# A convolution and a gated two-layer product on one core: the joins of the first product over both PSUM banks of a pair at once

## The chip, the cores and the metric

The kernel runs on one core of a Trainium2 chip. Five engines work side by side, each in the order of its own instruction list, and wait for each other through counters (semaphores): TensorE (PE, matrix products; its weight loads are listed apart as PEld), VectorE (DVE), ScalarE (ACT), GpSimd (POOL) and SyncE (SP), which here only starts transfers. PE writes its results into PSUM, which has eight banks of 512 fp32 values in each of 128 partitions. DVE and ACT read and write PSUM, and everything else lies in SBUF.

The metric is the device time of one execution in microseconds: the median of several runs. Lower is better.

## The reference

```python
# lightweight convolution: batch 8, sequence 4096, width 192, 8 heads of 24 channels, 7 taps
w = softmax(weight, axis=-1)                       # [8, 7]
x_pad = concatenate([zeros(B, 6, D), x], axis=1)
out[b, s, h*24+g] = sum_k w[h, k] * x_pad[b, s+k, h*24+g]
# two-layer product with a quick GELU, over all 32768 tokens
h = out.reshape(32768, 192) @ w_in                 # w_in [192, 2048]
g = h * (1 / (1 + exp(-1.702 * h)))
result = g @ w_out                                 # w_out [2048, 192]
```

All of it is fp32, and a matrix product of fp32 operands runs as two passes on PE, so each product is two records in the profile.

## The kernel before

The tokens are worked in 32 big steps. Each holds two column blocks of 512 tokens (one from each half of the batch). A big step has a first product (tokens by `w_in`, then the GELU) and a second product (the result by `w_out`). Both use schemes of the Strassen kind, which need fewer block products and pay with sums of blocks. Big step 0 is done by functions of its own (`first_step`, with `plain` and `second_first`) while the weights are still being loaded and rounded; big steps 1 to 31 all run through the same two functions, `hidden` (called twice, for `v` = 0 and 1) and `second`. Nothing is scheduled by a planner of times: the order of each engine's list is the order in which the code issues it (`manual_schedule`). The waits between engines are put in by the framework, from the tiles that each instruction reads and writes.

**PSUM.** The eight banks are eight tiles of 128x512: `slots`, three pairs, and `sums`, one pair. In the code a pair is a list of two tiles, one for each `h`. The names `x`, `y`, `z` and `sums` move round among the four pairs from step to step.

**First product** (`hidden`). `terms` calls `product1` (L616) 21 times for each `v`. Each call issues two matmuls, one into each bank of a pair; they use different halves of PE's rows and run together. Between them `copy2` (L653) copies a pair from PSUM to one of five SBUF buffers `k15`, `k16`, `k18`, `k19`, `k20` (all in the tile `room`) as two ACT copies, one for each bank. `sum2` (L657) joins a pair with one of these buffers: a VectorE sum or difference of two operands, done bank by bank as two operations of 128x512. There are six calls of `sum2` in each `hidden`: `x = z - k15`, `k15 = y - k19`, `k19 = z - k19`, `k20 = k20 + sums`, `k16 = y - k16`, `k18 = k18 + sums`. `gelu` writes the activation into the tile `g`: from a pair in PSUM as two operations (L638), from a buffer as one of 128x1024 (L642). Where `hidden` calls `work`, DVE does steps of the next token block's convolution (L502, L504); `sum_g` puts sums of blocks of `g` (L391, L393) on DVE.

**Second product** (`second`). `PLAN` lists it step by step. Here the two banks of a pair have different duties:

```python
mains, sides = (bs[0], bx[0], by[0]), (bx[1], bs[1], by[1])
```

A main product fills partitions 0 to 95 of a bank `mains[i]`, in three matmuls of 32 columns for every step of the sum; these are the values `p0` to `p5`, two to a bank. With every three of them goes one matmul of a side product, on PE's last 32 columns: it fills partitions 96 to 127 of a bank `sides[i]`. All four run together (`one_matmul`, L991). Seven side products of three chunks each make 21 side results, and each is copied to `room` by ACT as soon as its last matmul is done (L1016, 32x256). `seed` copies a main value to or from PSUM on ACT (L1020, 96x256), `join` adds or subtracts such values on DVE (L391, L393, 96x256), and `turn` transposes results into the output buffer (L908). So in this stage the bank with `h` = 0 of each pair holds main values and the bank with `h` = 1 side values.

**Big step 0.** `first_conv` (L1078) makes two thirds of the first convolution on PE in the pairs `slots[1]` and `slots[2]`, bank 0 for the first 512 tokens and bank 1 for the second. `take_straight` (L1092) and `take_across` (L1096) copy them out, and `split_rest` (L356, L357) follows on ACT on the way to the first rounded weights (L376). `second_first` uses the banks one by one, mains in `slots[1][0]`, sides in `sums[0]`, `sums[1]` and `slots[0][0]` (L822, L827; side copies L829).

Of the kernel before, what the change touches and what calls it, by code (L numbers as in the profile page):

```python
# [8 lines left out]
F32 = mybir.dt.float32  # L9
# [6 lines left out]
def kernel(  # L16
# [35 lines left out]
    P = 128  # L52
# [6 lines left out]
    TOK = 2 * T  # L59
# [17 lines left out]
    psum = ctx.enter_context(tc.tile_pool(name="psum", bufs=1, space=bass.MemoryType.PSUM))  # L77
# [9 lines left out]
    def load_x(big, ns=range(2)):  # L87
# [16 lines left out]
                    )  # L104


    slots = [
        [psum.tile([P, TOK], F32, name=f"slot{i}{h}") for h in range(2)] for i in range(3)
    ]
    sums = [psum.tile([P, TOK], F32, name=f"sums{h}") for h in range(2)]  # L110

# [534 lines left out]
    def bank(t, h):  # L648
        return t[h] if isinstance(t, list) else t[:, h, :]
# [3 lines left out]
            act.copy(bank(dst, h), bank(src, h))  # L653

    def sum2(op, dst, a, b):
        for h in range(2):
            op(*(bank(t, h) for t in (dst, a, b)))  # L657

    def plain(u, m, n, v, slot, ks=range(NC), first=0):

# [3 lines left out]
    def hidden(big, v, x, z, y, sums, work, fetch, last=lambda: None):  # L664
# [45 lines left out]

        pe(y, 6, 14, first=True)
        sum2(vec.tensor_sub, x, z, k15)
        early(1)
        if not v or big == 1:
# [6 lines left out]
        pe(z, 11)  # L721
        pe(sums, 20, 10)
        sum2(vec.tensor_sub, k15, y, k19)
        gelu(B12, 0, v, sums)
        pe(x, 4)
        copy2(k20, x)
        sum2(vec.tensor_sub, k19, z, k19)
        early(2)
        if not v or big == 1:
# [523 lines left out]
    for big in range(1, N_BIG):  # L1253
        more = big + 1 < N_BIG
        last = hidden(big, 0, x, z, y, sums, work, lambda: fetch(big, 1, z))
        x, z, y, sums = z, x, sums, y
# [39 lines left out]
```

## Time and profile before

| what | value |
|---|---|
| median of 3 runs | 2274.22 us (2273.69 to 2274.6) |
| profiled execution: span from the first to the last instruction | 2272.6 us; no other time is listed for it, and the median run is 1.6 us above the span |
| PE busy | 2263.4 us (100% of the span), granted clock 1.000 |
| DVE busy | 1941.0 us (85%) |
| ACT busy | 1568.8 us (69%) |
| POOL busy | 847.0 us (37%) |
| DMA | mean 125 GB/s |

Engines overlap, so the busy times don't add up. A row of a group of instructions gives the line, the engine, the operation, `written<-read` by tile names, shapes, count, then busy time, the mean in ns, and the idle time of the engine just before. A row of the timeline gives the start, the duration, engine, line, operation and count, and in brackets the engine's idle time before it with what ended it. All eight PSUM banks are called `slot` or `sums` there, without their numbers.

### The profile page before, as it was taken

The numbers are of one execution on the slowest core, as the hardware profiler recorded it, in microseconds if no ns is written. First come the engines' busy times: TensorE is split into PE (matmuls) and PEld (weight loads), VectorE is DVE, ScalarE is ACT, GpSimd is POOL, SyncE is SP. The second block draws the span as 40 slices with busy tenths as digits, with TensorE's granted clock in tenths as the row PEclk, the third lists the DMA queues.
The fourth block names the chain that finished last, engine by engine and source line by source line (L and its number), as shares of the span: only waits on it lengthen the run. The fifth ranks groups of instructions, "written<-read, shape, count | busy, mean of one in ns | idle before, by whom it ended". The sixth has DMA issues, their size and how long they took to land.

```text
span 2272.6 us, 60950 instructions
## 1 busy us (share of the span) xinstructions
PE 2263.4 (100%) x25214; PEld 1214.9 (53%) x25214; DVE 1941.0 (85%) x2794; ACT 1568.8 (69%) x2972; POOL 847.0 (37%) x834
## 2 busy tenths in 40 slices
PE   9999999999999999999999999999999999999998
PEld 5475555555555555555555555555555555555556
DVE  8998888888888888888888888888888888888877
ACT  8866776667766667666677666776667766667754
POOL 1544443244442344433444324444244442344400
PEclk9999999999999999999999999999999999999999
DMA  9976656656566665666655675656666566664443
GB/s 205 155 146 127 127 111 126 137 122 131 116 126 129 123 139 114 116 126 134 134 120 109 126 144 121 131 112 127 132 126 136 112 124 126 129 139 86 88 99 71
DMA packets 269908, 284.20 MB, mean 125 GB/s; under 512 B 117952, under 2 KB 206016, under 8 KB 269632
## 3 DMA queue, kind: packets, MB, share of 16 engines
q0 software_dynamic: 57648, 150.69, 36.9%
q1 hardware_dynamic: 210336, 129.22, 25.2%
q8 instruction: 199, 3.26, 0.6%
q14 instruction: 77, 0.63, 0.1%
q10 hardware_dynamic: 1648, 0.39, 0.1%
HBM read 53.15 MB, written 25.17 MB: 34 GB/s over the span
## 4 chain that ended last, share of the span: by engine, by line
PE 99%; DVE 1%; ACT 0%; DMA 0%; issue 0%; SPq 0%; ACTq 0%; DVEq 0%
PE slot L616 35%; PE slot L991 33%; PE sums L616 16%; PE sums L991 13%; PE slot L822 2%; DMA xin<-in_x_dram 0%; DVE room L657 0%; DVE xt L473 0%; ACT conv_t L1096 0%; DVE conv_t L504 0%; SPq L99 0%; ACT conv_t L357 0%; DVE room L393 0%; ACT conv_t L356 0%; DVE g L391 0%
## 5 line engine op out<-in xcount | busy, mean ns | idle before, releaser
L616 PE MATMUL slot<-conv_t,w_in_s 64*128 64x512 f32 x3740 | 862.5, 591 | 0.3 <-DVE w_in_s L376 0.3
L991 PE MATMUL slot<-g,w_form 128*32 128x256 f32 x7024 | 710.8, 379 | 0.4 <-DVE room L657 0.4
L616 PEld LDWEIGHTS slot<-conv_t,w_in_s 64*128 64x128 f32 x3740 | 377.6, 187 | 423.9 <-issue 347.7
L393 DVE TENSOR_TENSOR g<-g 128x1024 f32<-128x1024 f32 x372 | 448.9, 1234 | 3.2
L991 PEld LDWEIGHTS slot<-g,w_form 128*32 128x32 f32 x7024 | 375.7, 110 | 118.1 <-DVE room L657 0.9
L616 PE MATMUL sums<-conv_t,w_in_s 64*128 64x512 f32 x1660 | 408.3, 589 | 0.3 <-DVE w_in_s L376 0.3
L1016 ACT COPY room<-slot 32x256 f32<-32x256 f32 x434 | 159.3, 367 | 310.3 <-PE slot L991 309.2
L642 ACT ACTIVATE g<-room 128x1024 f32<-128x1024 f32 x310 | 325.7, 1077 | 67.9 <-DVE room L657 67.9
L991 PE MATMUL sums<-g,w_form 128*32 128x256 f32 x2648 | 368.8, 379 | 0.0
L991 PE MATMUL slot<-g,w_out_s 128*32 128x256 f32 x4080 | 318.8, 380 | 0.0
L967 POOL DMA_DIRECT2D g<-g x124 | 106.2, 857 | 496.6 <-PE slot L991 156.8
L616 PEld LDWEIGHTS sums<-conv_t,w_in_s 64*128 64x128 f32 x1660 | 172.1, 187 | 184.9 <-issue 140.0
L518 POOL TENSOR_TENSOR conv_t<-conv_t,g 128x512 f32<-128x512 f32 x180 | 262.2, 1457 | 16.3 <-POOL conv_t L518 3.0
L530 POOL DMA_DIRECT2D g<-g x120 | 105.5, 879 | 422.5 <-PE sums L991 128.7
L653 ACT COPY room<-slot 128x512 f32<-128x512 f32 x434 | 231.4, 601 | 38.5 <-PE slot L616 38.4
L516 ACT ACTIVATE g<-xt,cw 128x512 f32<-128x512 f32 x360 | 248.5, 730 | 2.2
L991 PEld LDWEIGHTS slot<-g,w_out_s 128*32 128x32 f32 x4080 | 164.7, 110 | 128.5 <-ACT g L638 22.7
L638 ACT ACTIVATE g<-slot 128x512 f32<-128x512 f32 x334 | 180.8, 598 | 45.4 <-PE slot L616 24.8
L991 PEld LDWEIGHTS sums<-g,w_form 128*32 128x32 f32 x2648 | 177.9, 110 | 37.6
L504 DVE SCALAR_TENSOR_TENSOR conv_t<-xt,cw,conv_t 128x512 f32<-128x512 f32 (+1 forms) x198 | 192.0, 970 | 4.6
L393 POOL TENSOR_TENSOR conv_t<-conv_t 128x256 f32<-128x256 f32 x180 | 181.9, 1024 | 9.4
L1016 ACT COPY room<-sums 32x256 f32<-32x256 f32 x217 | 79.6, 367 | 145.0 <-PE sums L991 142.5
(205 smaller groups left out, 2909.5 us busy)
## 6 DMA issues: line engine op xcount, KB each, us to landing
g<-g POOLq DMA_DIRECT2D x124, 512.0 KB, 5.8
xin<-in_x_dram SPq DMA_DIRECT2D x240, 180.0 KB, 4.3
conv_t<-conv_t SPq DMA_DIRECT2D x180, 192.0 KB, 3.1
g<-g POOLq DMA_DIRECT2D x120, 256.0 KB, 3.8
out_dram<-osbs SPq DMA_DIRECT2D x186, 128.0 KB, 4.9
g<-room POOLq DMA_DIRECT2D x31, 512.0 KB, 5.3
conv_t<-g POOLq DMA_DIRECT2D x60, 256.0 KB, 4.8
g<-osbs POOLq DMA_DIRECT2D x30, 512.0 KB, 4.7
```

The source lines that it names most:

```text
L393: eng.tensor_sub(v(dst), v(a), v(b))
L504: vec.scalar_tensor_tensor(out=dst, in0=src, scalar=tap, in1=dst, op0=ALU.mult, op1=ALU.add)
L516: act.mul(home, conv_src(big, c, k), cw[:, c, k : k + 1])
L518: nc.gpsimd.tensor_add(dst, dst, home)
L530: nc.gpsimd.dma_start(out=out, in_=src, accum_op=ALU.add)
L616: nc.tensor.matmul(slot[h], w_in_s[halves[h], a, v * P : (v + 1) * P], src, start=first, stop=True, skip_group_check=True,)
L638: act.activation(dst[:, :, h, :], src[h].rearrange("p (o t) -> p o t", o=2), AF.Gelu_apprx_sigmoid)
L642: act.activation(dst.rearrange("p o h t -> p h o t"), src.rearrange("p h (o t) -> p h o t", o=2), AF.Gelu_apprx_sigmoid,)
L653: act.copy(bank(dst, h), bank(src, h))
L967: nc.gpsimd.dma_start(out=spot(dst), in_=spot(a), accum_op=ALU.add)
L991: nc.tensor.matmul(dst, w, t, start=first, stop=last, skip_group_check=True)
L1016: act.copy(to, d)
```

## The change

Each PSUM pair becomes one tile of 128x2x512 that holds both banks. It is still a list of the two banks for all code that takes them one at a time, and has a view of both. `sum2` uses that view, and so issues one VectorE operation of 128x1024 where it issued two of 128x512.

```diff
-    slots = [
-        [psum.tile([P, TOK], F32, name=f"slot{i}{h}") for h in range(2)] for i in range(3)
-    ]
-    sums = [psum.tile([P, TOK], F32, name=f"sums{h}") for h in range(2)]
+    class Banks(list):
+
+        def __init__(self, name):
+            tile = psum.tile([P, 2, TOK], F32, name=name)
+            super().__init__(tile[:, h, :] for h in range(2))
+            self.both = tile[:, :, :]
+
+    slots = [Banks(f"slot{i}") for i in range(3)]
+    sums = Banks("sums")
...
     def sum2(op, dst, a, b):
-        for h in range(2):
-            op(*(bank(t, h) for t in (dst, a, b)))
+        op(*(t.both if isinstance(t, Banks) else t for t in (dst, a, b)))
```

The instructions of PE, ACT, POOL and SP stay the same in number and order. DVE loses one instruction for each call of `sum2` (2 x 6 calls in each of 31 big steps, 372 in all). What else changes is the list of waits: the tiles are now four in place of eight. Lines below the change move by 4 or 5 (L616 becomes L621, L657 becomes L661, L991 becomes L995).

## The prediction

> **What bounds the kernel.** I read the page's busy times and its chain first, then the busy times by stage, then the timeline of one big step.
>
> ```profile
> span 2272.6 us, 60950 instructions
> PE 2263.4 (100%) x25214; PEld 1214.9 (53%) x25214; DVE 1941.0 (85%) x2794; ACT 1568.8 (69%) x2972; POOL 847.0 (37%) x834
> ...
> PE 99%; DVE 1%; ACT 0%; DMA 0%; issue 0%; SPq 0%; ACTq 0%; DVEq 0%
> ```
> ```profile
> core 0: us, PE busy (x) PEld busy (x) DVE busy (x) ACT busy (x) POOL busy (x), PEclk, DMA share, GB/s
> 0.00:18.00 18.00, 15.43 (x154) 11.76 (x154) 12.24 (x36) 13.70 (x36) 3.12 (x16) 1.00 0.99 211
> 1006.26:1042.51 36.25, 36.25 (x172) 16.70 (x169) 30.75 (x41) 30.39 (x51) 18.58 (x17) 1.00 0.59 114
> 1042.51:1076.32 33.81, 33.81 (x627) 20.18 (x625) 30.06 (x44) 18.18 (x42) 7.73 (x9) 1.00 0.68 138
> ```
>
> The chain is PE for 99%. The last two rows are the two stages of one big step (first product, second product): PE is busy for 36.25 of 36.25 and 33.81 of 33.81 us. So the other engines are paced by PE. Two things follow: work saved on DVE can't shorten a big step, and any time for which PE is made to wait lengthens the run by just that, 31 times.
>
> **The fused joins on DVE.**
>
> ```profile
> core 0: us, DVE busy (x), PEclk, DMA share, GB/s
> 0.00:2272.60 2272.60, 466.76 (x744) 1.00 0.63 125
> ```
> ```profile
> L393 DVE TENSOR_TENSOR g<-g 128x1024 f32<-128x1024 f32 x372 | 448.9, 1234 | 3.2
> ```
>
> The 744 joins of L657 overlap slightly: 466.76 / 744 = 0.627 us of busy time each, so a pair costs 1.255. There is no 128x1024 operation with a PSUM operand in the trace. The nearest row is the SBUF sum of 128x1024, 1.234 us, and I take it. The upper end is what a pair costs now, 1.255; as a lower end I take a fifth less than the row, 1.0, since no row of that size is near it. The saving is then 372 x 0.02 = 8 us of DVE time, at most 372 x 0.25 = 93, and I price it at nothing: PE's own work covers it. If PE were not busy all the time, it would be a gain of that size at most.
>
> The join as one also starts later. It needs both halves of what it waits for, and ACT delivers these one after the other.
>
> ```profile
> 1028.07 1.08 ACT L638 ACTIVATE g<-slot 128x512 f32<-128x512 f32 x2 [0.69 <-issue]
> ...
> 1028.70 1.30 DVE L657 TENSOR_TENSOR slot<-slot,room 128x512 f32<-128x512 f32 x2 [1.01 <-ACT g L638]
> ...
> 1031.26 1.88 PE L616 MATMUL slot<-conv_t,w_in_s 64*128 64x512 f32 x8
> ...
> 1033.24 2.47 DVE L657 TENSOR_TENSOR room<-slot,room 128x512 f32<-128x512 f32 x4
> ...
> 1034.69 1.88 PE L616 MATMUL slot<-conv_t,w_in_s 64*128 64x512 f32 x8
> ```
>
> Now the first half starts at 1028.70, as soon as the first activation is done, and the pair ends at 1030.00. In one piece it starts at 1028.07 + 1.08 = 1029.15 and ends at 1030.38, 0.4 later. PE needs that slot at 1031.26, so 0.9 is left of 1.3. Behind it on DVE are queued the sums of `g` and then the four joins from 1033.24; the first two end at 1034.5 and PE needs their slot in the second half of the row from 1034.69, at 1035.55. With 0.4 to 0.6 of delay 0.4 is still left, more than the 0.19 of a weight load. Where PE's result is what the join waits for, nothing is later at all. I price the joins' delay at 0 and keep 0.2 us a big step as its upper end.
>
> **The tiles.** The second part of the diff is the larger one. The built order of the changed kernel, with its waits, has the waits by tile: whoever writes one bank of a pair waits for whoever reads the other, and the reverse. In the first product that changes nothing, since both banks are used by the same two operations. In the second product the two banks of a pair hold different things, mains and sides. I took the waits of one second product as the changed kernel has them, and looked up in the timeline of before when each awaited instruction ends. Eleven matmuls of L991 start there before what they would have to wait for has ended. Each is a stop of PE. They are of four kinds.
>
> *Five times, mains behind a side copy of their own pair.* The first and the last:
>
> ```profile
> 1045.79 0.38 PE L991 MATMUL sums<-g,w_form 128*32 128x256 f32 x1
> 1045.99 0.39 PE L991 MATMUL sums<-g,w_out_s 128*32 128x256 f32 x3
> ...
> 1046.24 0.37 ACT L1016 COPY room<-sums 32x256 f32<-32x256 f32 x1 [0.86 <-PE sums L991]
> 1046.62 0.35 ACT L1020 COPY slot<-slot 96x256 f32<-96x256 f32 x1
> ...
> 1046.65 0.38 PE L991 MATMUL slot<-g,w_form 128*32 128x256 f32 x1
> ...
> 1046.87 0.38 PE L991 MATMUL slot<-g,w_form 128*32 128x256 f32 x1
> ```
> ```profile
> 1072.77 0.38 PE L991 MATMUL sums<-g,w_form 128*32 128x256 f32 x1
> ...
> 1073.00 0.37 ACT L1016 COPY room<-slot 32x256 f32<-32x256 f32 x1 [0.59 <-PE slot L991]
> ```
>
> A side ends with the matmul of 1045.79. PE goes on at 1045.99 with mains in the other bank of the same pair. As one tile they wait for the copy, 1046.24 + 0.37 = 1046.61: 0.62 late. The last: 1073.37 against the group of 1072.77, 0.6. To that comes PE's restart. Before has such a stop in its first second product:
>
> ```profile
> 135.87 0.37 ACT L1020 COPY room<-slot 96x256 f32<-96x256 f32 x1
> ...
> 136.29 0.42 PE L991 MATMUL slot<-osbs,w_form 128*32 128x256 f32 x3
> ...
> 136.53 0.82 PE L991 MATMUL slot<-osbs,w_form 128*32 128x256 f32 x11
> ```
>
> The copy ends at 136.24, PE starts at 136.29, and its next pass comes 0.24 after that in place of the 0.21 to 0.22 elsewhere: 0.05 + 0.03 = 0.08. So 0.70 each, 5 x 0.70 = 3.5 us.
>
> *Once, the same with a copy that is late already.*
>
> ```profile
> 1044.28 0.38 PE L991 MATMUL sums<-g,w_form 128*32 128x256 f32 x1
> ...
> 1045.01 0.37 ACT L1016 COPY room<-slot 32x256 f32<-32x256 f32 x1
> ```
>
> The copy ends at 1045.38, and the mains of the group of 1044.28 need its pair: 1.1 + 0.08 = 1.2.
>
> *Twice, a side behind a seed copy that itself has to wait.* The copy of 1046.62 (`seed`) reads one bank of a pair whose other bank a side is still filling. As one tile it waits for the matmul of 1046.65, which ends at 1047.03, and ends at 1047.4; the next matmul of a side in that pair is that of 1046.87: 0.55 + 0.08, with its twin 1.3 together.
>
> *Three times, a side behind a join on DVE.*
>
> ```profile
> 1060.09 0.87 DVE L393 TENSOR_TENSOR room<-room,slot 96x256 f32<-96x256 f32 x2
> ...
> 1060.91 0.37 ACT L1016 COPY room<-slot 32x256 f32<-32x256 f32 x1 [0.47 <-PE slot L991]
> ...
> 1061.12 0.38 PE L991 MATMUL slot<-g,w_form 128*32 128x256 f32 x1
> ...
> 1062.01 0.41 DVE L391 TENSOR_TENSOR room<-sums,room 96x256 f32<-96x256 f32 x1
> ...
> 1062.63 0.38 PE L991 MATMUL sums<-g,w_form 128*32 128x256 f32 x1
> ...
> 1062.84 0.38 PE L991 MATMUL sums<-g,w_form 128*32 128x256 f32 x1
> ```
>
> The two joins of 1060.09 can start only after the copy of 1060.91, at 1061.28, and end at 1062.15; the side of 1061.12 waits for them, 1.0 + 0.08. The join of 1062.01 waits for the matmul of 1062.63 (1063.01) and ends at 1063.42; the side of 1062.84 waits, 0.6 + 0.08. The third is like the second. Together 2.5.
>
> Sum: 3.5 + 1.2 + 1.3 + 2.5 = 8.5 us for each second product; 31 of them, 264 us. What else waits on ACT, DVE and POOL for these comes later by no more than PE itself.
>
> Bounds: if the restart cost nothing and the three joins were covered, 11 stops become 8 of 0.6 and one longer by 0.5, 5.3 us or 165 in all; if two more of the 21 side copies came to stop PE, 8.5 + 1.4 + the 0.2 of the joins, 10.1 us or 313.
>
> **Big step 0.**
>
> ```profile
> 9.87 0.37 ACT L1092 COPY conv_t<-slot 128x256 f32<-128x256 f32 x1 [0.63 <-PE slot L1078]
> ...
> 10.52 0.51 ACT L356 ACTIVATE conv_t<-conv_t,bias 128x256 f32<-128x256 uint32 x1 [0.28 <-DVE conv_t L345]
> ...
> 13.14 3.70 PE L616 MATMUL slot<-conv_t,w_in_s 64*128 64x512 f32 x16
> ```
> ```profile
> 83.52 0.57 ACT L829 COPY room<-sums 32x512 f32<-32x512 f32 x1
> ```
>
> The copy of 9.87 takes the first 512 tokens out of a pair while PE fills its other bank until about 13.1; as one tile it waits for that, and the weights of L616 wait behind it on ACT (L356): up to 3 us, less what was to spare, 2.5. In `second_first` four copies like that of 83.52 become stops of about 1 us each, 4. Together 6.5, between 0 and 10.
>
> **Sum.** 2272.6 + 264 + 6.5 = 2543 for the span, and the runs' median stands 1.6 above the span: 2545 us, 12% slower.
>
> **Rivals.** *PE's clock falls.* Eleven stops in 34 us could make the throttle grant less. If a quarter of each second product ran at half clock, that is 31 x 33.81 / 4 = 262 us more: 2807. Against it: the stretch from 0 to 18 us has PE busy for 15.43 of 18.00, and its granted clock is 1.00. [...] 3%.
>
> *All side copies stop PE.* There are 21 in each second product. If the delays shift them against each other so that the other ten count too, 31 x 10 x 0.70 = 217 more: 2762. Against it: the stops delay mains and sides alike. 5%.
>
> *The waits are met in time, and the kernel is not slower.* This is so if the copies end before PE gets to the matmuls behind them. Then the most to be had is a few us of PE's idle time, 2272.6 - 2263.4 = 9.2, nearly all of it in the start; I set it at 2272. It decides at one place: the copy of 1046.24 would have to end 0.62 us sooner, that is before it starts. That the framework tells the two banks of a tile apart, so that no wait is added, comes to the same time, and the built order speaks against it. 4% for both.
>
> **Numbers.** The forecast has 88%. 2545 is its sum. Its bounds are 2274 + 165 + 0 = 2439 and 2274 + 313 + 10 = 2597; the low end takes covers that the timeline does not show, so I put it at 2490, and the high end at 2600. That leaves out the three rivals and little else. A measurement of this kernel tells about 0.2% from no change. Slower by over 0.2%: 96%; within 0.2%: 2%; faster: 2%.
>
> **What would show it.** Each big step takes 78.6 in place of 70.06 us, all of it in the second product, which goes from 33.8 to about 42.3; the first stays at 36.25. L1016 ACT copies and L391/L393 joins of 96x256 appear as what ends the idle time of PE and PEld on L991, 31 times each. PE's busy share falls to about 90%, at a granted clock of 1.00. The joins (L661) are 372 of about 1.23 us. Wrong would be the forecast if second products stayed near 34 us, if the first product grew, or if the clock dropped.

## The result, and the profile after

The changed kernel takes 2548.36 us (median of its runs, 2547.64 to 2550.05) against 2274.22 before: a ratio of 1.1207, with a 95% interval of 1.1191 to 1.1223. It is 12% slower; the forecast was 2545. One execution of a kernel told of below, the convolution laid out by token halves, took 4241.75 us at a mean granted clock of 0.556; it is left out of that kernel's median (2547.94 with it) and of its ratio.

The page of the kernel after, the lines that answer to those shown of before (span, busy times, shares of the chain by engine):

```profile
span 2546.1 us, 60733 instructions
PE 2377.6 (93%) x25214; PEld 1168.3 (46%) x25214; DVE 1952.7 (77%) x2422; ACT 1583.7 (62%) x2972; POOL 828.5 (33%) x834
...
PE 86%; ACT 6%; DVE 5%; issue 2%; DMA 1%; POOL 0%; ACTq 0%; DVEq 0%; POOLq 0%
```

DVE has 372 instructions fewer and PE as many as before. DVE's busy time still rose, from 1941.0 to 1952.7 us: the joins take less (below), but others of its operations take longer, such as the convolution steps (L504, now L509: a mean of 1039 ns in place of 970). Why was not followed up. The chain, 99% PE before, now goes over ACT and DVE for 11%: PE waits for them.

The busy times of the kernel after for the same stretches as in the prediction (the columns are those of its header: the stretch and its length, then busy us and instructions of PE, PEld, DVE, ACT, POOL, then the granted clock): the start, a first product, a second product.

```profile
0.00:18.00 18.00, 13.42 (x144) 10.95 (x146) 9.71 (x29) 11.41 (x32) 3.13 (x16) 1.00 0.99 211
...
1046.31:1082.56 36.25, 36.25 (x170) 16.09 (x171) 30.19 (x30) 30.55 (x51) 18.91 (x18) 1.00 0.54 107
1082.56:1124.94 42.38, 37.45 (x628) 20.32 (x626) 30.37 (x43) 18.50 (x42) 7.76 (x9) 1.00 0.56 114
```

The first product is what it was, 36.25 us and PE busy throughout. The second product went from 33.81 to 42.38. The start has 2.0 us less of PE's work done by 18 us. The granted clock is 1.00 in all three. So the loss is time in which PE is stopped: 8.57 us in each of 31 second products, 266 us, and 7.5 us by which the first second product begins later. Together that is 273.2 of the 273.5 us between the spans.

What ends each stop, from the timeline of the kernel after: the weight loads of PE in one second product ahead of which PE waited, with the idle time and its releaser in brackets.

```profile
1082.55 0.12 PEld L995 LDWEIGHTS slot<-g,w_out_s 128*32 128x32 f32 x3 [0.76 <-ACT g L643]
1085.42 1.45 PEld L995 LDWEIGHTS slot<-g,w_form 128*32 128x32 f32 x32 [1.42 <-ACT room L1020]
1087.84 0.12 PEld L995 LDWEIGHTS slot<-g,w_out_s 128*32 128x32 f32 x3 [0.97 <-ACT room L1020]
1089.38 0.11 PEld L995 LDWEIGHTS sums<-g,w_form 128*32 128x32 f32 x1 [0.53 <-ACT sums L1024]
1096.06 0.12 PEld L995 LDWEIGHTS sums<-room,w_form 128*32 128x32 f32 x3 [0.94 <-ACT room L1020]
1098.05 1.88 PEld L995 LDWEIGHTS slot<-g,w_form 128*32 128x32 f32 x40 [0.54 <-ACT room L1024]
1102.58 0.12 PEld L995 LDWEIGHTS sums<-g,w_out_s 128*32 128x32 f32 x3 [0.94 <-ACT room L1020]
1105.05 0.12 PEld L995 LDWEIGHTS slot<-osbs,w_form 128*32 128x32 f32 x3 [1.02 <-ACT room L1020]
1107.58 0.11 PEld L995 LDWEIGHTS slot<-g,w_form 128*32 128x32 f32 x1 [1.08 <-DVE room L398]
1110.01 0.14 PEld L995 LDWEIGHTS slot<-g,w_form 128*32 128x32 f32 x2 [0.97 <-DVE room L396]
1111.14 0.11 PEld L995 LDWEIGHTS slot<-g,w_form 128*32 128x32 f32 x1 [0.88 <-DVE room L398]
1121.28 1.45 PEld L995 LDWEIGHTS slot<-g,w_form 128*32 128x32 f32 x32 [0.94 <-ACT room L1020]
```

The first row is the entry from the first product and was there before. The other eleven are the stops: six behind a side copy (L1020), two behind a seed copy (L1024), three behind a join (L396, L398). The idle time in brackets is not what the stop costs: at the first of the eleven it is 1.42 us and the stop costs 1.12, at that of 1096.06 it is 0.94 and the stop costs 1.04. The cost of a stop is read from the starts of successive groups of four matmuls, which follow each other every 0.43 us where nothing waits (two passes, as from 1083.00 over 1083.22 to 1083.43).

The list of waits for the whole run shows that this holds in all 31 second products (columns: total us, times, longest). For the side copies:

```profile
PEld slot L995 <- ACT room L1020: 133.9, 124, 2.4
...
PEld sums L995 <- ACT room L1020: 60.1, 62, 1.3
```

124 + 62 = 186 = 6 x 31. In the same list the waits of PEld on L995 for a seed copy (L1024) number 31 + 16 + 15 = 2 x 31, and those for a join (L396 and L398) 47 + 15 + 16 + 15 = 3 x 31.

The joins as one operation: two of their five groups in the kernel after (count, then busy us and mean ns; the means of all five are 1211 to 1232), and the busy time of all of them together (the stretch and its length, then DVE's busy us and number of operations):

```profile
L661 DVE TENSOR_TENSOR slot<-slot,room 128x1024 f32<-128x1024 f32 x62 | 76.4, 1232 | 70.2 <-ACT g L643 70.2
...
L661 DVE TENSOR_TENSOR room<-room,slot 128x1024 f32<-128x1024 f32 x62 | 75.1, 1211 | 38.1 <-PE slot L621 37.9
```
```profile
0.00:2546.10 2546.10, 448.21 (x372) 1.00 0.56 112
```

That is 448.21 us in place of 466.76. So the fusion saved 18.6 us of DVE time on the joins in the whole run, and the tiles that it needs cost 274 us.

### The profile page after: what moved, and what is told of

The parts are those of the page before. It is cut to its first block, busy times and chain, and to the rows that moved or that the text cites. A ratio compares the mean times of both kernels' runs of the same rounds, so it can differ in the third digit from the quotient of the medians.

```text
span 2546.1 us, 60733 instructions
## 1 busy us (share of the span) xinstructions
PE 2377.6 (93%) x25214; PEld 1168.3 (46%) x25214; DVE 1952.7 (77%) x2422; ACT 1583.7 (62%) x2972; POOL 828.5 (33%) x834
## 4 chain that ended last, share of the span: by engine, by line
PE 86%; ACT 6%; DVE 5%; issue 2%; DMA 1%; POOL 0%; ACTq 0%; DVEq 0%; POOLq 0%
PE slot L621 30%; PE slot L995 28%; PE sums L995 14%; PE sums L621 13%; ACT room L1020 3%; DVE room L661 2%; DVE room L398 2%; ACT g L647 1%; DVE room L396 1%; DMA w_form<-w_form 1%; ACT room L1024 0%; DMA w_form<-w_out_s 0%; PE slot L826 0%; DMA xin<-in_x_dram 0%; PE slot L1082 0%
## 5 line engine op out<-in xcount | busy, mean ns | idle before, releaser
L621 PE MATMUL slot<-conv_t,w_in_s 64*128 64x512 f32 x3740 | 857.0, 591 | 2.9 <-DVE w_in_s L381 2.5
L995 PE MATMUL slot<-g,w_form 128*32 128x256 f32 x7024 | 748.9, 381 | 79.6 <-ACT room L1020 44.1
L621 PEld LDWEIGHTS slot<-conv_t,w_in_s 64*128 64x128 f32 x3740 | 357.5, 187 | 446.7 <-issue 355.8
L995 PEld LDWEIGHTS slot<-g,w_form 128*32 128x32 f32 x7024 | 353.9, 110 | 292.5 <-ACT room L1020 74.0
L398 DVE TENSOR_TENSOR g<-g 128x1024 f32<-128x1024 f32 x372 | 455.6, 1252 | 9.5 <-ACT g L647 6.3
L1020 ACT COPY room<-slot 32x256 f32<-32x256 f32 x434 | 159.1, 367 | 415.3 <-PE slot L995 370.8
L995 PE MATMUL sums<-g,w_form 128*32 128x256 f32 x2648 | 391.8, 381 | 14.0 <-DVE room L396 7.4
L621 PE MATMUL sums<-conv_t,w_in_s 64*128 64x512 f32 x1660 | 403.5, 589 | 1.0 <-ACT room L658 0.7
L995 PE MATMUL slot<-g,w_out_s 128*32 128x256 f32 x4080 | 330.1, 382 | 14.6 <-ACT room L1020 14.6
L658 ACT COPY room<-slot 128x512 f32<-128x512 f32 x434 | 231.3, 600 | 38.4 <-PE slot L621 38.3
L621 PEld LDWEIGHTS sums<-conv_t,w_in_s 64*128 64x128 f32 x1660 | 159.2, 186 | 198.5 <-issue 145.9
L995 PEld LDWEIGHTS sums<-g,w_form 128*32 128x32 f32 x2648 | 172.4, 110 | 91.3 <-DVE room L396 14.6
L509 DVE SCALAR_TENSOR_TENSOR conv_t<-xt,cw,conv_t 128x512 f32<-128x512 f32 (+1 forms) x198 | 205.7, 1039 | 4.6
L1020 ACT COPY room<-sums 32x256 f32<-32x256 f32 x217 | 79.4, 366 | 202.7 <-PE sums L995 160.0
L995 PEld LDWEIGHTS slot<-g,w_out_s 128*32 128x32 f32 x4080 | 153.7, 109 | 94.6 <-ACT room L1020 29.5
L995 PE MATMUL slot<-osbs,w_form 128*32 128x256 f32 x1624 | 158.6, 380 | 8.7 <-ACT room L1020 8.7
```

The lines of the kernel that those rows point to most:

```text
L398: eng.tensor_sub(v(dst), v(a), v(b))
L509: vec.scalar_tensor_tensor(out=dst, in0=src, scalar=tap, in1=dst, op0=ALU.mult, op1=ALU.add)
L621: nc.tensor.matmul(slot[h], w_in_s[halves[h], a, v * P : (v + 1) * P], src, start=first, stop=True, skip_group_check=True,)
L995: nc.tensor.matmul(dst, w, t, start=first, stop=last, skip_group_check=True)
L1020: act.copy(to, d)
```

## The experiments

The theory: the time is lost by waits between the two banks of a pair that has become one tile, in the second product, and the wide join itself is worth next to nothing. The rivals: the wide join, or its later start, does harm by itself; large tiles cost something in general, whatever stands in which bank; PE's clock gives way.

### One part of the change at a time

The tiles merged, and the joins still bank by bank (against the kernel after):

```diff
     def sum2(op, dst, a, b):
-        op(*(t.both if isinstance(t, Banks) else t for t in (dst, a, b)))
+        for h in range(2):
+            op(*(bank(t, h) for t in (dst, a, b)))
```

> The pairs are one tile each, as in the changed kernel, but the joins stay two operations of 128x512. If the added waits between the banks of a pair are the cause (theory), nothing is better than in the changed kernel: 2549 us, 2540 to 2560, with second products of 42.4 us and 744 joins of about 0.63 us. If the longer join is the cause (rival), the time goes back to 2274.

Measured: 2551.67 us, ratio to before 1.1219 (1.1203 to 1.1234). A second product of this kernel:

```profile
534.30:576.76 42.46, 37.47 (x628) 20.35 (x626) 30.43 (x44) 18.57 (x42) 7.76 (x9) 1.00 0.57 114
```

The tiles alone bring the whole loss. The wide join on top of them doesn't do harm. If anything it helps by 0.07 us a second product (42.46 against 42.38), some 2 us in 31 of them; the intervals of the two runs overlap, so this is no more than likely.

The other way round: the separate tiles of before, and the joins cut finer still, in four operations of 128x256 for a pair (against the kernel before):

```diff
     def sum2(op, dst, a, b):
         for h in range(2):
-            op(*(bank(t, h) for t in (dst, a, b)))
+            for c in (slice(0, T), slice(T, TOK)):
+                op(*(bank(t, h)[:, c] for t in (dst, a, b)))
```

> The kernel before with each join in four operations of 128x256 in place of two of 128x512. From the 96x256 joins of 0.41 us this adds about 0.25 us to each of 372 joins, 93 us of DVE time. By the theory PE covers it: 2274 to 2282. If DVE's time set the end (rival), 2367, and then the fused join would have had something to give.

Measured: 2276.19 us, ratio 1.0010 (1.0001 to 1.0019). The busy time of all its joins, as above:

```profile
0.00:2274.20 2274.20, 527.42 (x1488) 1.00 0.63 125
```

The joins take 61 us more of DVE than before (93 were expected), and the run is 2 us longer. These 2 us lie in the start: the first second product begins at 132.27 in place of 130.43, and behind it the two products of a big step take 36.25 and 33.81 us as before. DVE's work on the joins is covered by PE in both directions: 61 us more cost 2, and the 18.6 us less could never have gained much.

### Which bank a side product gets

If the loss comes from what shares a pair with what, another assignment of the side products to the same banks must change it by an amount that can be worked out. Two such assignments, against the kernel after:

```diff
-        mains, sides = (bs[0], bx[0], by[0]), (bx[1], bs[1], by[1])
+        mains, sides = (bs[0], bx[0], by[0]), (by[1], bx[1], bs[1])
```

> The changed kernel with other pairings: each side product lies in the pair of another main product (sides in by[1], bx[1], bs[1] in place of bx[1], bs[1], by[1]). Work and order of all engines are the same. By the theory the time follows the number of matmuls whose new wait ends after their turn. Looked up in the timeline of before, that is 18 in a second product in place of 11, 13.9 us in place of 8.6: 2274 + 31 x 13.9 + 10 to 20 in the first steps = 2720, 2690 to 2750. If it were a cost that a pair as one tile has wherever the banks lie (rival), 2548.

```diff
-        mains, sides = (bs[0], bx[0], by[0]), (bx[1], bs[1], by[1])
+        mains, sides = (bs[0], bx[0], by[0]), (bs[1], by[1], bx[1])
```

> The changed kernel with the third rotation of the sides (bs[1], by[1], bx[1]). Looked up in the timeline of before, 16 matmuls of a second product stop, 11.6 us in all. Theory: 2274 + 31 x 11.6 + 7 to 14 = 2644, 2620 to 2665. Rival (a cost of the pair as such): 2548.

And the first of them with the separate tiles of before, by the same line:

> The control to the other pairings: the kernel before, eight tiles, with the sides in the same banks as in the run with turned sides. By the theory the place alone costs little: one wait a step may come late (the turned side bank meets the copies at the stage's end), 0 to 0.9 us a step, 2274 to 2302. If the place of the banks were itself what costs (rival), it would be 2720 here too.

With the first of these assignments (in one tile or apart) the last side product sums in a bank that is already being refilled for the next big step, so the last side chunk and the values kept for the next step become others, and these two kernels don't compute the reference's result; only their times are used. The instructions are the same in number and size.

Measured: 2728.0 us (ratio 1.1994, 1.1972 to 1.2016), 2650.97 (1.1658, 1.1635 to 1.1681), and apart 2301.71 (1.0119, 1.0105 to 1.0133). A second product of each, in this order:

```profile
646.18:694.46 48.28, 39.43 (x627) 20.54 (x625) 30.94 (x44) 18.18 (x42) 7.77 (x9) 1.00 0.52 105
```
```profile
548.55:594.29 45.74, 39.15 (x627) 20.53 (x626) 30.39 (x44) 18.19 (x42) 8.59 (x10) 1.00 0.56 112
```
```profile
486.19:520.93 34.74, 34.42 (x626) 20.28 (x624) 30.34 (x45) 18.20 (x42) 7.73 (x9) 1.00 0.69 138
```

The same tiles and the same instructions give 42.38, 45.74 or 48.28 us, by nothing but which bank a side product is put in. Over the 33.81 of before that is 14.47 us more for the first assignment and 11.93 for the second, where 13.9 and 11.6 had been worked out from the timeline of before. With separate tiles the turn costs 0.93 us (34.74 against 33.81), and with merged ones 5.90. A cost of large tiles in general would have left all three alike. It falls.

### One pair apart

`sums` as two tiles again; the joins that touch it go bank by bank, the others stay wide (against the kernel after):

```diff
-    sums = Banks("sums")
+    sums = [psum.tile([P, TOK], F32, name=f"sums{h}") for h in range(2)]
...
     def sum2(op, dst, a, b):
-        op(*(t.both if isinstance(t, Banks) else t for t in (dst, a, b)))
+        if any(isinstance(t, list) and not isinstance(t, Banks) for t in (dst, a, b)):
+            for h in range(2):
+                op(*(bank(t, h) for t in (dst, a, b)))
+        else:
+            op(*(t.both if isinstance(t, Banks) else t for t in (dst, a, b)))
```

> The changed kernel with one of the four pairs (the one that starts as sums) as two tiles again; a join that touches it is two operations of 128x512, the others stay one of 128x1024. The names move round, so each second product has 2 or 3 of its three pairs as one tile. Theory: about two thirds of the stops stay, 31 x 5.9 + 7 = 190: 2465, 2440 to 2490. Rival (the length of the join): the share of fused joins falls to about a half, which would give about 2410.

Measured: 2464.75 us, ratio 1.0839 (1.0818 to 1.0861). Two second products that follow each other:

```profile
516.30:555.84 39.54, 36.48 (x627) 20.49 (x625) 30.30 (x44) 18.39 (x42) 7.74 (x9) 1.00 0.60 123
...
592.09:632.13 40.04, 36.43 (x627) 20.37 (x625) 30.20 (x43) 18.41 (x42) 7.80 (x9) 1.00 0.61 125
```

They alternate, since `sums` changes its place among the pairs from step to step. The stops are a property of single pairs: with one of four apart about 30% of the loss is gone (39.5 and 40.0 in place of 42.38), and of the eleven stops in the list of PE's weight loads seven and eight are left.

### The awaited copy made longer

Each side copy made twice, one after the other, in the kernel after and in the kernel before (L1020 and L1016):

```diff
                 if to is not False:
                     act.copy(to, d)
+                    act.copy(to, d)
```

> The changed kernel with each of the 21 side copies of a second product made twice, one behind the other (same values, 0.36 us more of ACT for each). Theory: a stop is the end of the side's matmul, the copy and PE's restart, so each stop that a side copy ends grows by 0.36: six stops of PE and one of the joins in each second product, 31 x 2.5 = 78, and up to 30 more where a wait was just met before: 2627, 2610 to 2665. If the stops came from something else than the copies (rival), 2549 to 2560.

> The control: the kernel before with the side copies made twice. ACT gets 21 x 0.36 = 7.6 us more in a second product, where it is busy for 18.2 of 33.8 us. Theory: no matmul waits for a side copy that comes right before it, so PE goes on: 2274, up to 2285 if one of the later waits is met too late. If ACT's time itself were close to setting the end (rival), 2300 and more.

Measured: 2657.68 us after (1.1687, 1.1664 to 1.1711), which is 109 more than without the second copy; 2294.22 before (1.0089, 1.0072 to 1.0106), 20 more. Second product of the first; then first and second product of the other:

```profile
551.84:597.69 45.85, 37.77 (x626) 20.03 (x625) 30.45 (x43) 25.77 (x63) 7.76 (x9) 1.00 0.53 106
```
```profile
448.50:485.08 36.58, 36.58 (x173) 23.60 (x169) 30.24 (x42) 31.25 (x53) 19.65 (x18) 1.00 0.60 118
485.08:519.21 34.13, 34.12 (x625) 20.00 (x625) 29.84 (x44) 24.91 (x61) 7.63 (x9) 1.00 0.65 132
```

In both kernels ACT gets 21 x 0.367 = 7.7 us more to do in a second product. Before, that costs PE 0.32 us there and 0.33 us in the first product. This misses the expectation of 2274 to 2285. The timeline has three places where ACT is now late: a seed copy (0.08), a join behind another seed copy (0.20), and the copy that prepares the next first product (L653), whose second bank comes 0.33 late. After, it costs 3.47 us, all in the second product (45.85 against 42.38). The timeline has the same eleven stops as above. Two of their rows in this kernel, the first side copy and the first join, and two rows that are new in the list:

```profile
555.11 0.12 PEld L995 LDWEIGHTS slot<-g,w_form 128*32 128x32 f32 x3 [1.82 <-ACT room L1021]
...
570.80 1.43 PEld L995 LDWEIGHTS slot<-g,w_form 128*32 128x32 f32 x26 [0.24 <-ACT room L1025]
...
579.33 1.02 PEld L995 LDWEIGHTS slot<-g,w_form 128*32 128x32 f32 x24 [1.48 <-DVE room L398]
...
589.10 0.12 PEld L995 LDWEIGHTS slot<-g,w_out_s 128*32 128x32 f32 x3 [0.46 <-DVE slot L396]
```

The first and the third row stood at 1.42 and 1.08. By the starts of the groups, the seven stops behind a side copy (six that end with one, and the first join, which starts after one) cost 0.22 to 0.40 more each, 2.41 together. The rest of the 3.47 is a join that seeds (the last row, 0.34 more), two stops behind seed copies that were met in time without the second copies (0.15 and 0.13, and 0.05 in the passes behind them), and the entry to the next first product, which comes 0.40 later behind L658 on ACT. So the same copies stand in PE's way in the one kernel and hardly in the other: the second copy costs 3.47 us a big step there and 0.65 here.

### The start

The convolution of big step 0 with its two token halves in the two pairs, so that each pair holds what is copied out together (against the kernel after):

```diff
-                        slots[c][n][halves[h], 0:T],
+                        slots[1 + n][c - 1][halves[h], 0:T],
...
-        over(conv_t[:, c - 1, 2 * c + n, :], slots[c][n][:, 0:T])
+        over(conv_t[:, c - 1, 2 * c + n, :], slots[1 + n][c - 1][:, 0:T])
...
-            over(conv_t[halves[1 - h], 2 - c, 2 * c + n, :], slots[c][n][halves[h], 0:T])
+            over(conv_t[halves[1 - h], 2 - c, 2 * c + n, :], slots[1 + n][c - 1][halves[h], 0:T])
```

> The changed kernel with the first convolution on PE laid out by the other way: the banks of one pair hold one half of the tokens, so that no copy out of a pair has to wait for the other half's matmuls. Theory: the first big step is 1.5 to 3 us shorter than in the changed kernel, 2546 us; the rest is the same. Rival (the start is set by the load of the weights): no difference, 2548.

The kernel after ran once more beside it:

> The changed kernel beside the others on the same chip: 2548.

Measured: 2547.50 us (1.1202, 1.1183 to 1.1221), and 2549.03 (1.1209, 1.1190 to 1.1228) for the kernel after. The 1.5 us between them are not resolved by these intervals. The trace shows the step itself. First the kernel after, then this one:

```profile
13.07 0.37 ACT L1096 COPY conv_t<-slot 128x256 f32<-128x256 f32 x1 [3.80 <-PE slot L1082]
...
15.52 2.77 PE L621 MATMUL slot<-conv_t,w_in_s 64*128 64x512 f32 x10 [2.12 <-DVE w_in_s L381]
```
```profile
10.12 0.37 ACT L1096 COPY conv_t<-slot 128x256 f32<-128x256 f32 x1 [0.91 <-PE slot L1082]
...
13.04 2.85 PE L621 MATMUL slot<-conv_t,w_in_s 64*128 64x512 f32 x12
...
16.41 1.13 PE L621 MATMUL slot<-conv_t,w_in_s 64*128 64x512 f32 x4 [0.52 <-DVE conv_t L1096]
```

The copy that began at 9.87 before began at 13.07 after, and the first product at 15.52 in place of 13.14. With the halves rearranged they are back at 10.12 and 13.04. By the start of the first second product 1.3 us of these 2.5 are left: later waits in the start, such as that of 16.41, take the rest.

No kernel among these beats the one before.

## Why the prediction was right

**PE bounds, the other engines are paced by it.** Right. The first product is 36.25 us to the hundredth, and 61 us more of work on DVE cost 2.

**The joins priced at nothing.** Right. The operation measures 1.21 to 1.23 us, where 1.23 was taken from the sum of 128x1024 in SBUF, and the DVE time saved is 18.6 us, where 8 were worked out. Their later start shows nowhere: no first product grew. The means of single operations would have promised more: they are 679 to 695 ns by group for a narrow one before and 1211 to 1232 for the wide one, so that a pair would save 0.14 to 0.16 us, group by group. But the operations overlap in this trace: by busy time a pair took 1255 ns before and 448.21 / 372 = 1205 after, so the saving was 0.05 us, about a third of that. Neither is worth anything where PE does not wait for the joins.

**Waits by tile.** Right, and it is the heart of it. The stops are not a demand of PSUM. In the kernel before the same copies ran beside the same matmuls, in 33.81 us: while the side copy of 1046.24 took its 0.37 us, the mains of 1046.20 and 1046.42 went into the other bank of its pair, 0.22 apart as elsewhere.

**Eleven stops of 8.5 us.** Eleven were found, of the kinds and numbers that were named, and 8.57 us in sum. The terms were further off than the sum. From the starts of the groups of matmuls, the same in every steady second product to 0.01 us:

| kind | predicted | measured |
|---|---|---|
| six behind a side copy | 1.2 + 5 x 0.70 = 4.7 | 1.12, 0.67, 1.04, 1.04, 0.72, 0.79 = 5.38 |
| two behind a seed copy | 1.3 | 0.23, 0.25 = 0.48 |
| three behind a join | 1.08 + 0.68 + 0.7 = 2.5 | 0.79, 0.77, 0.60 = 2.16 |
| others | 0 | 0.23 behind a join that seeds, and 0.32 left, nearly all of it (0.024 each) in the pass after each stop |

The five of 0.70 each were sized by the first and the last of them, and those two are nearly right (0.67, 0.79). Two in between are longer, and the timeline of the kernel after shows one of them:

```profile
1094.80 0.38 PE L995 MATMUL sums<-osbs,w_form 128*32 128x256 f32 x1
1094.81 0.39 PE L995 MATMUL slot<-room,w_form 128*32 128x256 f32 x3
1095.02 0.59 PE L995 MATMUL sums<-osbs,w_form 128*32 128x256 f32 x2
1095.65 0.36 ACT L1020 COPY room<-sums 32x256 f32<-32x256 f32 x1 [1.36 <-PE sums L995]
...
1096.06 0.42 PE L995 MATMUL sums<-room,w_form 128*32 128x256 f32 x3 [0.46 <-ACT room L1020]
```

The side's last two passes run alone from 1095.02, while its mains have ended: here the side runs two passes behind, its end is later by as much, and so is the copy. The stop counts from 1095.02, when the next group was due, to 1096.06. The seed copies were priced from the wrong end:

```profile
1097.19 0.38 PE L995 MATMUL slot<-g,w_form 128*32 128x256 f32 x1
1097.38 0.61 PE L995 MATMUL sums<-room,w_form 128*32 128x256 f32 x6
1097.63 0.37 ACT L1024 COPY room<-slot 96x256 f32<-96x256 f32 x1 [1.62 <-PE slot L995]
```

The copy waits for the side's pass of 1097.19 and ends at 1098.00, but mains in another pair (x6) are ahead of the stopped matmul in PE's list and run meanwhile, until 1097.99. The prediction had no work between. The errors are +0.7, -0.8, -0.3 and +0.5, and that they cancel is luck; each kind alone was good to some 15% but for the seeds.

**The restart.** 0.08 was 0.05 from the end of the copy to PE's start and 0.03 in the pass behind. The trace gives 0.051 to 0.055 for the first, in all second products alike, and 0.024 for the second.

**Big step 0.** 6.5 was priced, and the first second product begins 7.5 us later than before (137.90 against 130.43). Its first term, 2.5, measures 2.4 (15.52 against 13.14). Its second, 4 in `second_first`, measures 3.9: from its first main matmul to its last it takes 40.72 us in place of 36.86. There it was not four stops of 1 us: the mains stop three times, for 1.67, 1.26 and 0.83. What is left, 0.7 between the two and 0.5 behind them, was not priced.

**PE's busy share.** Predicted about 90%, measured 93%. This was wrong in the reading, not in the time: of the 8.57 us that a second product lost, only 42.38 - 37.45 = 4.93 appear as idle. The rest counts as busy, 37.45 in place of 33.81: in a flow a pass starts every 0.22 us and each matmul's 0.38 us are overlapped by those behind it, while the last one ahead of a stop is shown in full. So the share of busy time shows little more than half of what these short stops cost.

**The clock.** Right in every steady step: with eleven stops in 42 us the granted clock is 1.00 in the second product shown above, and no matmul of L995 into a `slot` takes over 404 ns in the whole run (median 379). The forecast's 2807 for this rival rested on the author's own guess of a quarter of each second product at half clock, which no trace shows; what the traces show is a few stretches at 0.52 to 0.60 in the start, told below.

**The rivals.** Of the 21 side copies six stop PE, as forecast, and not all; none of the eleven waits is met in time.

## What to carry to other kernels

Before two PSUM banks are put in one tile for the sake of one wider operation, list what else lives in them: if PE fills one bank while another engine empties the other, any such copy can become a stop of PE (here 6 of 21 side copies did), and the price is read by laying each awaited end of the old timeline beside the start of the matmul behind it. Here 18.6 us of saved DVE time were bought with 274 us of PE. Fewer operations on an engine that PE doesn't wait for gained some 2 us at most here, and cutting them finer cost 2.

## What the runs showed that was not expected

The granted clock gave way in the start of kernels with merged tiles, in some executions and not in others: twice in the second run of the kernel after, to 0.53 and 0.60 in the stretches below, in the run with the tiles alone to 0.52 (143.40 to 146.80), and not in the first run of the kernel after. In that second run the longest matmul into a `slot` takes 1125 ns in a first product and 634 in a second one, in the first run 693 and 404. Among the kernels with separate tiles, the traces of the one before, of the turned sides and of the joins in quarters also have 693 and 404 as their longest; for the one with the copies made twice it was not measured. The busy times of the kernel after in its second run, and then of its first run in the same stretches:

```profile
16.30:19.70 3.40, 3.40 (x10) 1.43 (x10) 3.04 (x9) 3.28 (x8) 0.00 (x0) 0.53 1.07 229
142.00:146.00 4.00, 3.53 (x40) 1.53 (x44) 3.96 (x4) 0.37 (x1) 0.00 (x0) 0.60 1.07 242
```
```profile
16.30:19.70 3.40, 3.24 (x14) 0.99 (x12) 3.02 (x8) 3.28 (x8) 0.00 (x0) 1.00 1.06 228
142.00:146.00 4.00, 3.47 (x62) 1.64 (x55) 3.96 (x5) 1.07 (x3) 0.00 (x0) 1.00 1.05 238
```

By an estimate from these rows each of the two stretches could cost up to 1.6 us (3.40 x 0.47, 4.00 x 0.40). The first one cost next to nothing, since the first second product begins at 137.9 in both runs. The second one can account for most of the 1.8 us by which the span of that run is longer (2547.9 against 2546.1). Both stretches follow a longer stop of PE, of 2.12 us ahead of 15.50 and 2.00 us ahead of 141.94. But the first run has such stops at the same two places (2.12 and 1.88 us), at a clock of 1.00, so that the stop alone doesn't decide. In the steady steps of the kernel after, where no stop of PE costs over 1.2 us, it was not seen. What decides was not tried.
